# Eight w1 half tiles instead of six, two ReLU tiles instead of one, and raw w1 tiles asked for earlier

## The chip, the cores and the metric

The kernel runs on one core of one Trainium2 chip. The metric is the device time of one execution in microseconds (us), from several runs; the profile is of one execution. The core's engines are TensorE (PE; PEld is its weight load), VectorE (DVE), ScalarE (ACT), GpSimd (POOL) and SyncE (SP), which issues every DMA of this kernel.

## The reference

The input x has 2048 tokens of 512 features. It is normalised, goes through attention with 32 heads of 16 features and, in parallel, through an MLP with 1792 hidden features and squared ReLU, and the two are joined by a gate:

```python
xn = _layernorm(x)
qkv = (xn @ wqkv)                                  # 32 heads of 16
p = softmax(einsum("bhqd,bhkd->bhqk", q, k) * 16 ** -0.5)
s = (p @ v) @ wo
h = relu(einsum("bsd,df->bsf", xn, w1) + b1)       # 1792 hidden
g = silu(einsum("bsf,fd->bsd", h * h, w2) + b2)
return x + s * g
```

All of it is in float32.

## The kernel before, in words

Operands of the large products are split into a high and a low part in a shorter float format (`split`), and each product is the sum of three matmuls, high by high, high by low and low by high (`terms3`). 

Attention goes in 32 units: 8 groups of four heads by 4 blocks of 512 queries. A unit has 16 steps, one for each block of 128 keys, so the main loop has 512 steps, numbered `st`. In a step TensorE makes four score tiles (`exp_mm`, L1123) whose exponentials ScalarE takes (L1130), four score tiles for the row maxima of the unit 24 steps ahead (`max_mm`, L289), each reduced by VectorE (L296), and the P·V product of the step two before (`pv_mm`, L362), which closes the step. The row maxima go through DRAM into two rows of the q tile as a shift (`keep`, `back`). When a unit is done its result is copied out (`evac`, L372), its row sums are gathered by a DMA into a small tile sm (L380), inverted by VectorE (L386), sent through DRAM as a broadcast (L389, L394) and multiplied in by GpSimd (L400 to L402). These six actions stand 1, 4, 5, 7, 9 and 12 steps after the copy.

The MLP is the filling of these steps: the generator `dense()` hands out, step by step, a list of matmuls. It works in 8 chunks of 256 tokens. For each chunk there are 14 tiles of 128 hidden features (`first`, two steps each, in chunk 0; `first_pair`, four steps for two tiles, in chunks 1 to 7), then two token tiles of the second product (`second`, 14 steps each). So the first product of chunk 0 runs in steps 4 to 31, its second product in 32 to 59, and each later chunk takes 56 steps. The results of the first product go through the tile `r`: ScalarE writes the ReLU of two hidden tiles into its halves (L490, L532), GpSimd squares it in place (L493, L535) and splits it into hT (L80, L81). `gate` in `second` uses the same memory for the tanh (`th`, L559 to L561). PSUM has one bank for the MLP (`pd`, one buffer), so a tile's first matmul waits until ScalarE has taken the tile before.

w1 reaches the chip in two ways. In chunk 0 each of the 14 tiles comes as a raw tile (`load_w1`, L433) in a ring of three tiles called ex, is split by GpSimd into two half tiles of the ring w1s (`split_w1`), and stored split in DRAM two steps later (L445). In chunks 1 to 7 the split half tiles come back from DRAM (`load_part`, L455), 28 a chunk. The ring w1s has six half tiles. Six are loaded ahead during the second product of the chunk before; the others are asked for inside `first_pair`, each at the place in TensorE's order where the half tile whose place it takes has been read for the last time (`between`). The raw tiles of w2 use the ring ex after those of w1 (`load_w2`).

In the main loop the order on each engine is the program's order, nothing is reordered. `later(n, fn)` puts an action at the beginning of the step n steps on, and `begin(st)` runs those that are due, ahead of the step's other work. SP issues in order, so a DMA that waits holds up all that stand behind it: the q tiles (L134), the k tiles (L145), the shift rows (L335, L355), the sums, w1, w2 and the MLP's outputs (L563).

Of the kernel before, what the change touches and what calls it, by code (L numbers as in the profile page):

```python
# [8 lines left out]
F32 = mybir.dt.float32  # L9
F32R = mybir.dt.float32r  # L10
# [6 lines left out]
P = 128  # L17
# [22 lines left out]
def kernel(  # L40
# [55 lines left out]
    with ExitStack() as ph:  # L96
# [317 lines left out]
        def mlp_tasks(mp):  # L414
# [4 lines left out]
            rot["ex"] = [ex.tile([P, D], F32, name=f"ex{i}") for i in range(3)]  # L419
            turn["ex"] = 0  # L420
            m1 = ExitStack()
            r = m1.enter_context(tc.tile_pool(name="rp", bufs=1)).tile([P, 2, CW], F32, name="r")
            wr = m1.enter_context(tc.tile_pool(name="wr", bufs=1))
            xp = m1.enter_context(tc.tile_pool(name="xc", bufs=1))
            w2t = wp.tile([P, 2, FO, D], F32R, name="w2t")
            rot["w1s"] = [wr.tile([P, 2, 2, P], F32R, name=f"w1s{i}") for i in range(6)]
            turn["w1s"] = 0

            raws = []
# [46 lines left out]
            def first(c, fo):  # L476
                i = fo % 2
                if fo == 0:
                    state["hT"] = hp.tile([P, 2, FO, CW], F32R, name="hT")
                xc, hT, w = state["xc"], state["hT"], state["w"].pop(0)  # L480
                ps = pd.tile([P, 512], F32, name="pd_t")[:, :CW]
                if fo + 2 < FO:
                    split_w1(fo + 2)
                if fo + 3 < FO:
                    load_w1(fo + 3)
                if fo >= FO - 5:
                    load_w2(fo - FO + 5, 3)

                def post():
                    nc.scalar.activation(r[:, i], ps, AF.Relu, bias=b1_t[:, fo : fo + 1])  # L490
                    if i == 0:
                        return
                    nc.gpsimd.tensor_tensor(r, r, r, op=ALU.mult)  # L493
                    fs = slice(fo - 1, fo + 1)
                    split((hT[:, 0, fs], hT[:, 1, fs]), r)

                return halves(
                    terms3(ps, [
                        (
                            lambda a, q, ko=ko: w[ko // 2][q, a, ko % 2],  # L500
                            lambda b, q, ko=ko: xc[q, b, ko],
                        )
                        for ko in range(KO)
                    ]), (12,), post, 2,
                )

            def first_pair(c, f):

                if f == 0:
                    state["hT"] = hp.tile([P, 2, FO, CW], F32R, name="hT")  # L510
                xc, hT = state["xc"], state["hT"]
                ps = pd.tile([P, 512], F32, name="pd_t")
                mms = []
                for i in range(2):
                    w = state["w"].pop(0)
                    mms += terms3(ps[:, i * CW : (i + 1) * CW], [
                        (
                            lambda a, q, ko=ko, w=w: w[ko // 2][q, a, ko % 2],
                            lambda b, q, ko=ko: xc[q, b, ko],
                        )  # L520
                        for ko in range(KO)
                    ])

                out_, lh, rh, _, last = mms[3 * KO]
                mms[3 * KO] = out_, lh, rh, False, last

                between = {k: load_part for k in (2, 5, 8, 11)}

                def post():
                    for i in range(2):  # L530
                        fo = 2 * f + i
                        nc.scalar.activation(  # L532
                            r[:, i], ps[:, i * CW : (i + 1) * CW], AF.Relu, bias=b1_t[:, fo : fo + 1]
                        )
                    nc.gpsimd.tensor_tensor(r, r, r, op=ALU.mult)  # L535
                    fs = slice(2 * f, 2 * f + 2)
                    split((hT[:, 0, fs], hT[:, 1, fs]), r)

                return block(mms, 2, post, between)

            def second(c, tt):
                hT = state["hT"]
                ps = pd.tile([P, D], F32, name="pd_t")
                u = up.tile([P, D], F32, name="u")
                th = r.rearrange("p a b -> p (a b)")
                ts_ = slice(tt * P, (tt + 1) * P)

                if c == 0 and tt == 0:
                    for k in range(5, FO):
                        later(k - 4, lambda k=k: load_w2(k, 2))  # L550

                def post():
                    nc.scalar.activation(u, ps, AF.Copy)  # L553
                    nc.gpsimd.tensor_tensor(u, u, b2_t, op=ALU.add)  # L554
                    later(2, gate)

                def gate():

                    nc.scalar.activation(th, u, AF.Tanh, scale=0.5)  # L559
                    nc.gpsimd.tensor_scalar(th, th, 0.5, 0.5, op0=ALU.mult, op1=ALU.add)  # L560
                    nc.gpsimd.tensor_tensor(u, u, th, op=ALU.mult)  # L561
                    t0 = c * CW + tt * P
                    later(4, lambda: nc.sync.dma_start(g_d[t0 : t0 + P, :], u))  # L563

                mms = terms3(ps, [
                    (lambda a, q, fo=fo: hT[q, a, fo, ts_], lambda b, q, fo=fo: w2t[q, b, fo])
                    for fo in range(FO)
                ])
                if c == 0:
                    yield from halves(mms, (6,) * 7, post, 1)  # L570
                    return
                if c == NCK - 1 and tt:

                    for i, task in enumerate(halves(mms, (6,) * 7, post, 1)):
                        if i == 4:
                            oldest_first("pt")
                            rot["pt"][:] = [t for t in rot["pt"] if all(t is not x for x in rot["ex"])]
                        yield task
                    return

                if tt:
                    yield from halves(mms[:6], (6,), None, 1)
                    mms = mms[6:]
                for k in range(0, 36, 12):
                    yield from block(mms[k : k + 12], 1, post if tt and k == 24 else None)
                if not tt:
                    yield from halves(mms[36:], (6,), post, 1)
# [4 lines left out]
                load_w1(fo)  # L592
            state["w"] = []
            split_w1(0)
            later(1, lambda: split_w1(1))
            for _ in range(2):
                yield [], None
            for c in range(NCK):
                if c == 1:

                    oldest_first("pt")
                    rot["pt"][:0] = rot["ex"]
                if c == 0:
                    for fo in range(FO):
                        yield from first(c, fo)
                else:
                    for f in range(FO // 2):
                        yield from first_pair(c, f)
                if c + 1 < NCK:
                    load_xc(c + 1)  # L610
                    state["part"] = 0
                    for k in range(6):
                        later(14 + k, load_part)
                else:
                    m1.close()
                    wo_setup()
                for tt in range(CW // P):
                    yield from second(c, tt)
# [292 lines left out]
        def qk_tile(m, c, last=False):  # L911
            ps = pd.tile([P, 512], F32, name="pd_t") if last else pe.tile([P, 512], F32, name="se")
            for out_, lh, rh, first_, last_ in qk_terms(m, c, ps):
                nc.tensor.matmul(out_, lh(slice(0, P)), rh(slice(0, P)), start=first_, stop=last_)  # L914
                if not last_:
                    yield
            if last:

                hl = pools["n"].tile([P, 2, 512], F32R, name="hl")
                raw = sp.tile([P, 512], F32, name="ot", bufs=1)  # L920
                nc.scalar.activation(raw, ps, AF.Copy)
                split((hl[:, 0], hl[:, 1]), raw)
                later(3, lambda: qk_store(m, c, hl))
                yield
                return
            if m % 4 == 0:
                hl = hlp.tile([P, 2, 512], F32R, name="hl")
                split_psum(hl[:, 0], hl[:, 1], ps)
            else:
                hl = hlp.tile([P, 2, 512], F32R, name="hl")  # L930
                raw = hlp.tile([P, 512], F32, name="raw", bufs=2)
                nc.scalar.activation(raw, ps, AF.Copy)
                split((hl[:, 0], hl[:, 1]), raw)
            qk_store(m, c, hl)
            yield
# [388 lines left out]
```

## Time and profile before

| | us |
|---|---|
| median of three runs | 1696.4 |
| lowest and highest run | 1695.42, 1696.55 |
| the profiled execution's own time | 1695.05 |
| its span, first to last instruction | 1693.3 |

| engine | busy us | share of the span |
|---|---|---|
| TensorE matmul | 1660.9 | 98% |
| TensorE weight load | 943.8 | 56% |
| VectorE | 1353.3 | 80% |
| ScalarE | 1192.6 | 70% |
| GpSimd | 519.0 | 31% |

Busy time is the union of an engine's instructions. Matmuls are pipelined and their ends are modelled, so a busy TensorE can still have lost time; a wait shows in the idle time ahead of an instruction and in the distance between the closing groups of two steps. In a timeline a row gives the start in us from the beginning of the span, the duration, the engine (SPq is SyncE's queue of DMA issues), the line, what is written from what, how many, and in brackets the idle time before it with what ended it. The duration of an issue on SP is not that of its transfer; the chain of waits shows transfers from issue to landing where somebody waited for them.

### The profile page before, as it was taken

How to read it: one execution, taken by the hardware profiler on the slowest of the kernel's cores; microseconds unless marked ns; L12 is line 12 of the kernel's file. 1: busy time of each engine (PE TensorE's matmuls, PEld its weight loads, DVE VectorE, ACT ScalarE, POOL GpSimd, SP SyncE). 2: the span in 40 equal slices, each digit the busy share in tenths (PEclk: the TensorE clock that was granted, in tenths of full speed). 3: DMA queues.
4: the chain of work that ended last, by engine and by line, in shares of the span. 5: the costliest groups of instructions: out<-in, count | busy, mean ns of one | idle time of the engine just before them, and what ended most of it. 6: DMA issues, size and time to landing. Idle time of an engine off the chain costs nothing.

```text
span 1693.3 us, 35473 instructions
## 1 busy us (share of the span) xinstructions
PE 1660.9 (98%) x13312; PEld 943.8 (56%) x13312; DVE 1353.3 (80%) x2303; ACT 1192.6 (70%) x2354; POOL 519.0 (31%) x538
## 2 busy tenths in 40 slices
PE   6999999999999999999999999999999999999998
PEld 5766565556545655565466456545655565555533
DVE  6255688888888888888888888888888888887633
ACT  7211577777777777777777777777777777776675
POOL 4335467522212321231133113211221233134322
PEclk9999999999999999999999999999999999999999
DMA  7648566425333433343343334323432352158434
GB/s 281 176 148 269 163 188 191 110 78 139 104 77 92 116 95 86 99 118 80 90 118 94 78 86 142 106 59 97 139 91 76 75 151 72 42 183 231 120 111 137
DMA packets 156315, 207.73 MB, mean 123 GB/s; under 512 B 50992, under 2 KB 70960, under 8 KB 154608
## 3 DMA queue, kind: packets, MB, share of 16 engines
q1 hardware_dynamic: 156144, 205.46, 42.6%
q8 instruction: 105, 1.72, 0.5%
q14 instruction: 66, 0.54, 0.1%
HBM read 149.04 MB, written 56.08 MB: 121 GB/s over the span
## 4 chain that ended last, share of the span: by engine, by line
PE 94%; DMA 2%; DVE 1%; ACT 1%; POOL 1%; issue 0%; SPq 0%; ACTq 0%; DVEq 0%; POOLq 0%
PE po L362 29%; PE pm_t L289 17%; PE pd_t L236 16%; PE se L1123 13%; PE pd_t L204 9%; PE se L914 5%; PE se L945 3%; DMA w1s<-w_d 1%; PE pm_t L814 1%; DVE mx L296 1%; ACT pt L1130 0%; PE pm_t L326 0%; PE pm_t L1123 0%; DMA xc<-xn_d 0%; ACT xn L980 0%
## 5 line engine op out<-in xcount | busy, mean ns | idle before, releaser
L296 DVE TENSOR_REDUCE mx<-pm_t 128x1 f32<-128x512 f32 x2048 | 1275.6, 684 | 241.4 <-PE pm_t L289 142.4
L1130 ACT ACTIVATE pt<-se 128x512 f32<-128x512 f32 x1730 | 902.8, 610 | 258.1 <-PE se L1123 221.5
L289 PE MATMUL pm_t<-ka,qm 64*128 64x512 f32 x2048 | 797.5, 423 | 1.9 <-DVE mx L296 1.6
L1123 PE MATMUL se<-qe,ka 64*128 64x512 f32 x2000 | 686.4, 402 | 0.0
L362 PE MATMUL po<-pt,v 128*32 128x512 f32 x3556 | 545.1, 605 | 0.0
L289 PEld LDWEIGHTS pm_t<-ka,qm 64*128 64x128 f32 x2048 | 352.6, 184 | 276.5 <-DVE mx L296 249.1
L1123 PEld LDWEIGHTS se<-qe,ka 64*128 64x128 f32 x2000 | 339.5, 184 | 21.6 <-issue 5.7
L236 PEld LDWEIGHTS pd_t<-xc,w1s 64*128 64x128 f32 x2352 | 292.4, 187 | 86.4 <-issue 82.2
L236 PE MATMUL pd_t<-xc,w1s 64*128 64x256 f32 x2352 | 333.7, 288 | 2.2 <-DMA w1s<-w_d 2.0
L236 PE MATMUL pd_t<-w2t,hT 64*128 64x512 f32 x936 | 259.9, 410 | 0.0
L236 PEld LDWEIGHTS pd_t<-w2t,hT 64*128 64x128 f32 x936 | 156.1, 184 | 72.3 <-issue 65.4
L362 PE MATMUL po<-ex,v 128*32 128x512 f32 x540 | 192.3, 605 | 0.0
L1130 ACT ACTIVATE ex<-se 128x512 f32<-128x512 f32 x270 | 147.7, 614 | 37.1 <-PE se L1123 30.6
L535 POOL TENSOR_TENSOR r<-r 128x512 f32<-128x512 f32 x49 | 51.0, 1041 | 335.6 <-ACT r L532 335.6
L362 PEld LDWEIGHTS po<-pt,v 128*32 128x32 f32 x3556 | 79.9, 108 | 132.4 <-issue 111.3
L554 POOL TENSOR_TENSOR u<-u,b_t 128x512 f32<-128x512 f32 x16 | 20.6, 1285 | 310.5 <-ACT u L553 310.5
L204 PE MATMUL pd_t<-w2t,hT 64*128 64x512 f32 x408 | 105.5, 391 | 0.0
L204 PE MATMUL pd_t<-wot,oc 64*128 64x512 f32 x336 | 91.0, 407 | 2.9 <-ACT pt L1130 0.9
L400 POOL TENSOR_TENSOR ot<-ot,hl 128x512 f32<-128x512 f32 x30 | 38.5, 1285 | 179.8 <-DMA hl<-r_d 137.1
L204 PEld LDWEIGHTS pd_t<-wot,oc 64*128 64x128 f32 x336 | 58.9, 185 | 47.7 <-DVE mx L296 12.5
L204 PEld LDWEIGHTS pd_t<-w2t,hT 64*128 64x128 f32 x408 | 72.5, 184 | 8.9
L532 ACT ACTIVATE r<-pd_t,b_t 128x256 f32<-128x256 f32 x98 | 41.1, 470 | 51.6 <-PE pd_t L236 51.6
(115 smaller groups left out, 1113.1 us busy)
## 6 DMA issues: line engine op xcount, KB each, us to landing
w1s<-w_d SPq DMA_DIRECT2D x196, 256.0 KB
qm<-q_d SPq DMA_DIRECT2D x384, 32.0 KB
qe<-q_d SPq DMA_DIRECT2D x384, 32.0 KB
ka<-k_d SPq DMA_DIRECT2D x96, 128.0 KB
xn_d<-xT SPq DMA_DIRECT2D x8, 1024.0 KB
k_d<-hl SPq DMA_DIRECT2D x32, 256.0 KB
q_d<-hl SPq DMA_DIRECT2D x32, 256.0 KB
xc<-xn_d SPq DMA_DIRECT2D x16, 512.0 KB
```

What stands on the lines that cost most here:

```text
L204: mm = nc.tensor.matmul(out_, lh(r), rh(r), start=first_ and lane == 0, stop=last_ and lane == 1, skip_group_check=True,)
L236: mm = nc.tensor.matmul(out_, lh(r), rh(r), start=first_ and lane == 0, stop=last_ and lane == 1, skip_group_check=True,)
L289: nc.tensor.matmul(ps, qms[u][p][64 * j : 64 * j + 64, qb * P : (qb + 1) * P], kas[qd, p][64 * j : 64 * j + 64, kc * 512 : (kc + 1) * 512] ...
L296: return nc.vector.tensor_reduce(mxs[u][:, c, kc : kc + 1], ps, axis=AX.X, op=ALU.max)
L362: nc.tensor.matmul(po[32 * j : 32 * j + 32, :], vs[qd][:, (4 * kb + j) * VW : (4 * kb + j) * VW + 32], pts[j], start=(kb == 0), stop=(kb = ...
L400: nc.gpsimd.tensor_tensor(ot, ot, hl[:, 1].bitcast(F32), op=ALU.mult)
L532: nc.scalar.activation(r[:, i], ps[:, i * CW : (i + 1) * CW], AF.Relu, bias=b1_t[:, fo : fo + 1])
L535: nc.gpsimd.tensor_tensor(r, r, r, op=ALU.mult)
L914: nc.tensor.matmul(out_, lh(slice(0, P)), rh(slice(0, P)), start=first_, stop=last_)
L945: nc.tensor.matmul(out_, lh(slice(0, P)), rh(slice(0, P)), start=first_, stop=last_)
L1123: nc.tensor.matmul(se, kas[qd, j // 2][b : b + 64, kb * P : (kb + 1) * P], qes[u][j // 2][b : b + 64, :], start=True, stop=True,)
L1130: return nc.scalar.activation(pts[j], se, AF.Exp, scale=0.25)
```

## The change

There are five edits. The tile `r` becomes two tiles `rs`, used in turn by the pairs of hidden tiles, and by the two token tiles in `gate`. The ring w1s has eight half tiles; eight are asked for ahead, at steps 13 to 20 after the second product begins, instead of six at steps 14 to 19. Inside `first_pair` nothing is edited: the loads there stop by themselves when all 28 are asked for. In chunk 0 a raw tile of w1 is asked for five tiles ahead instead of three, directly behind the split that frees its place; tiles 3 and 4 are asked for one and two steps after the first split. The store of the last k tile, which is computed at the beginning of the main loop, moves from three to six steps after its computation.

```diff
-            r = m1.enter_context(tc.tile_pool(name="rp", bufs=1)).tile([P, 2, CW], F32, name="r")
+            rp = m1.enter_context(tc.tile_pool(name="rp", bufs=1))
+            rs = [rp.tile([P, 2, CW], F32, name=f"r{i}") for i in range(2)]
...
-            rot["w1s"] = [wr.tile([P, 2, 2, P], F32R, name=f"w1s{i}") for i in range(6)]
+            rot["w1s"] = [wr.tile([P, 2, 2, P], F32R, name=f"w1s{i}") for i in range(8)]
...
-                ps = pd.tile([P, 512], F32, name="pd_t")[:, :CW]
+                ps, r = pd.tile([P, 512], F32, name="pd_t")[:, :CW], rs[fo // 2 % 2]
                 if fo + 2 < FO:
                     split_w1(fo + 2)
-                if fo + 3 < FO:
-                    load_w1(fo + 3)
+                if fo + 5 < FO:
+                    load_w1(fo + 5)
...
-                xc, hT = state["xc"], state["hT"]
+                xc, hT, r = state["xc"], state["hT"], rs[f % 2]
...
-                th = r.rearrange("p a b -> p (a b)")
+                th = rs[tt].rearrange("p a b -> p (a b)")
...
-            later(1, lambda: split_w1(1))
+            later(1, lambda: [split_w1(1), load_w1(3)])
+            later(2, lambda: load_w1(4))
...
-                    for k in range(6):
-                        later(14 + k, load_part)
+                    for k in range(8):
+                        later(13 + k, load_part)
...
-                later(3, lambda: qk_store(m, c, hl))
+                later(6, lambda: qk_store(m, c, hl))
```

## The prediction

> **What bounds the kernel now.** I read the page first, then busy time by stretch, then what TensorE waited for in those stretches, and at the end the timeline around each wait. The page's first lines and its chain of waits:
>
> ```profile
> span 1693.3 us, 35473 instructions
> PE 1660.9 (98%) x13312; PEld 943.8 (56%) x13312; DVE 1353.3 (80%) x2303; ACT 1192.6 (70%) x2354; POOL 519.0 (31%) x538
> PE 94%; DMA 2%; DVE 1%; ACT 1%; POOL 1%; issue 0%; SPq 0%; ACTq 0%; DVEq 0%; POOLq 0%
> ```
>
> The chain that ended last is TensorE's own work for 94%. An edit that takes no matmul away can win only what TensorE waits. The diff reaches two stretches: the MLP's first chunk (195 to 290 us), and chunks 1 to 7 (366 to 1412 us). In the table by stretch each engine has its busy us; the last three columns are the granted clock, DMA share and GB/s:
>
> ```profile
> 195.00:290.00 95.00, 90.88 (x852) 56.07 (x856) 79.57 (x133) 71.25 (x141) 64.10 (x91) 1.00 0.63 191
> 366.00:1412.00 1046.00, 1043.78 (x9214) 585.01 (x9206) 922.46 (x1546) 803.56 (x1602) 253.17 (x250) 1.00 0.38 100
> ```
>
> What weight loads (PEld) waited for in the first stretch (first row) and in the second (second row): us in total, times, longest:
>
> ```profile
> PEld pd_t L204 <- ACT r L490: 4.2, 2, 2.3
> PEld pd_t L236 <- DMA w1s<-w_d: 4.0, 5, 1.1
> ```
>
> These 4.2 and 4.0 us are the stake, 8.2 us or 0.48% of the span. The larger sums in the same view (waits for VectorE's maximum, for issue) come from the interleaving of every step, which the diff leaves alone.
>
> Is a wait of TensorE lost time, or slack that is made up later? The P·V group (L362) closes each step; these are its starts around the first 2.3 us wait, the first three rows from TensorE's timeline, the other two from the chain in order of time:
>
> ```profile
> 213.37 1.06 PE L362 MATMUL po<-pt,v 128*32 128x512 f32 x8
> 216.23 1.07 PE L362 MATMUL po<-pt,v 128*32 128x512 f32 x8
> 221.37 1.06 PE L362 MATMUL po<-pt,v 128*32 128x512 f32 x8
> ...
> 224.29 1.01 PE po L362 x8
> 227.20 1.00 PE po L362 x8
> ```
>
> Steps last 2.86 us before, 5.14 with the wait, then 2.92 and 2.91. Nothing is made up, so a wait that goes is worth its length. The Trainium skill's Perfetto Trace Analysis, section Identifying the Most-Contended Engine, calls matmul busy time no measure for TensorE and takes LDWEIGHTS busy time instead. By that rule 56% of the span here would make VectorE, at 80%, the most contended engine, and the gain from these waits would be near zero instead of 8.2 us. The steps after the wait do not bear that out.
>
> **The change part by part.**
>
> First chunk: the raw w1 tiles and the second ReLU tile. The timeline around both 2 us waits, in order of time (idle time and its releaser in brackets):
>
> ```profile
> 209.81 0.55 SPq L433 DMA_DIRECT2D ex<-in_B_w_dram  x1
> 213.73 0.40 POOL L80 TENSOR_SCALAR w1s<-ex 128x256 fp32r<-128x256 f32 x1 [7.93 <-DMA ex<-in_B_w_dram]
> 216.10 1.04 POOL L493 TENSOR_TENSOR r<-r 128x512 f32<-128x512 f32 x1
> 217.92 1.26 POOL L81 TENSOR_TENSOR hT<-r,hT 128x512 fp32r<-128x512 f32 x1
> 219.22 0.47 ACT L490 ACTIVATE r<-pd_t,b_t 128x256 f32<-128x256 f32 x1 [2.22 <-POOL hT L81]
> 219.74 0.18 PEld L204 LDWEIGHTS pd_t<-xc,w1s 64*128 64x128 f32 x1 [2.33 <-ACT r L490]
> ...
> 279.08 0.47 ACT L490 ACTIVATE r<-pd_t,b_t 128x256 f32<-128x256 f32 x1 [1.78 <-POOL hT L81]
> ```
>
> Raw tile 3 is asked for at 209.81, so GpSimd stands 7.93 us before it can split it; the squaring of the first pair queues behind that split, its last reader of r ends at 219.18, and only then may ScalarE write the next ReLU into the same r. The PSUM bank has one buffer, so TensorE waits with it. The second wait has the same end but another start: GpSimd, busy for 64 of this stretch's 95 us, is behind with splits of w1 and w2 and with the normalisation of a finished unit.
>
> With two r tiles in turn, ReLU 2 writes the other tile and does not wait for the first pair; ReLU 12 waits for the pair before last, whose split of hT stands four steps (11 us) earlier. That alone removes both waits: -4.2 us. What is late next is the consumer of hT, the second matmul, which begins after the chunk and reads the last pair in the last of its seven parts; a lag of GpSimd of a few us there costs nothing. Without that cover GpSimd's backlog would be paid in full, 1.8 us.
>
> Raw tile 3 now goes out a step after the first split. Ahead of it on SP stand these:
>
> ```profile
> 200.95 5.71 SPq L134 DMA_DIRECT2D qm<-q_d  x12
> 206.76 2.01 SPq L900 DMA_DIRECT2D k_d<-hl  x2
> 208.86 0.90 SPq L445 DMA_DIRECT2D w_d<-w1s  x2
> ```
>
> It goes behind the first six of the twelve qm loads, at 200.95 + 2.85 = 203.8, and with the 213.73 - 209.81 = 3.9 us that it took before it lands near 207.7, 6 us sooner. The two w1s tiles it needs are the two added ones. The k_d store moves three steps back and its 2.01 us with it; its readers come five head groups later. I count nothing extra for this: the same 4.2 us go either way.
>
> The cost: each later raw load (L433, five ahead) now takes the place of the tile split in the same step, so SP stands until GpSimd has finished that split, and everything behind it on SP stands too. The tightest thing behind it is the sum row of the first finished unit (sm, L380), which VectorE's reciprocal needs at a fixed place in its order:
>
> ```profile
> 239.03 0.44 SPq L433 DMA_DIRECT2D ex<-in_B_w_dram  x1
> 241.71 0.73 POOL L81 TENSOR_TENSOR w1s<-ex,w1s 128x256 fp32r<-128x256 f32 x1
> 240.19 2.68 SPq L134 DMA_DIRECT2D qe<-q_d  x6
> 243.39 2.62 SPq L134 DMA_DIRECT2D qm<-q_d  x6
> 246.11 2.67 SPq L445 DMA_DIRECT2D w_d<-w1s  x2
> 248.87 0.62 SPq L380 DMA_DIRECT2D sm<-ot  x1
> 251.36 0.24 DVE L386 RECIPROCAL sm<-sm 128x16 f32<-128x16 f32 x1
> 1544.86 1.91 DMA sm<-ot
> ```
>
> The row of 1544.86, from the chain, is the only one that shows how long such a transfer takes when VectorE stands waiting: 1.91 us. In the first chunk it has 251.36 - 248.87 = 2.49 us, a slack of 0.6. After the change the raw load of 239.03 waits for the split that ends at 241.71 + 0.73 = 242.44, 3.4 us later. Behind it: the load and a ka load (0.5 us each), six qe (2.7), six qm (2.6), two w1 stores (0.90 as at 208.86, or 2.67 as here) put sm at 249.7 to 251.5 and its landing at 251.6 to 253.4 (the first wait's 2.3 us shift all of this alike). VectorE then waits 0.2 to 2.0 us. Below that lies 0, if SP made up the rest; I take 1.0, since the short store is the commoner row, and charge it to TensorE in full, though three PSUM banks for the maxima can hide some. The shift rows of units 1 and 2 stand behind the same waits, but are needed six steps (17 us) after they are asked for, against SP waits like these 3.4 us. Cost: +1.0 (0 to 2.0).
>
> Chunks 1 to 7: eight half tiles. SP's timeline ahead of one of the five waits, then that wait, and two of the four w1s transfers of such length that stand in the chain, the first and the longest:
>
> ```profile
> 706.21 2.75 SPq L134 DMA_DIRECT2D qm<-q_d  x6
> 709.78 1.84 SPq L455 DMA_DIRECT2D w1s<-w_d  x4
> 712.60 0.18 PEld L236 LDWEIGHTS pd_t<-xc,w1s 64*128 64x128 f32 x1 [1.04 <-DMA w1s<-w_d]
> ...
> 709.78 2.78 DMA w1s<-w_d
> 1077.89 3.39 DMA w1s<-w_d
> ```
>
> SP issues without a gap from 706.2 to 711.6 (q tiles of the next unit), so the half tile whose place came free in the third step of the pair goes out at 709.78 and lands 2.78 us later, 1.04 too late. With six tiles it is wanted as third half of the next pair, some two steps (6 us) after its place is free; with eight as first half of the pair after, some five and a half steps (16 us). Ten us more against a lateness of at most 1.1 us removes all five waits: -4.0 us. The number of loads stays 28 a chunk: eight instead of six ahead, none instead of two in the sixth pair. The two added ones stand at the ends of this stretch of SP, shown for chunk 3's loads:
>
> ```profile
> 642.91 0.42 SPq L455 DMA_DIRECT2D w1s<-w_d  x1
> 651.57 2.91 SPq L134 DMA_DIRECT2D qe<-q_d  x6
> ```
>
> SP is idle from 643.3 to 651.6, so an issue of 0.42 us is free there; the other end is after the qm loads, with the next unit's need steps away. Zero, at most 2 x 0.42 us a chunk if SP were full. The two r tiles change nothing here: GpSimd is busy 253 of 1046 us.
>
> Sum: -4.2 - 4.0 + 1.0 = -7.2 us on the profiled execution's 1695.05, which gives 1687.9. That execution lies 1.3 us under the median of the runs, 1696.4; I predict 1696.4 - 7.2 = 1689.2 us.
>
> **The rivals.** *Half of it stays.* Either the w1s loads are still late, or GpSimd's lag still reaches TensorE. For it: SP stays the one queue of all loads. Against it: the margins above, 10 us against 1.1, and a second tile against a single dependence. It gives 1696.4 - 4.2 + 1.0 = 1693.2, or with the other half 1693.4.
>
> *Waits are slack.* VectorE is busy 922 of 1046 us in the second stretch and takes the waits' place; 1696.4. For it: 88% is not far from full. Against it: the steps after the wait. The Trainium skill's rule above leads here too.
>
> *Slower, by SP's queue in the first chunk.* If SP, standing behind the raw loads, falls so far behind that the sum row and the shift rows come late, VectorE and then TensorE stand. The seven even-numbered tiles each have such a wait of about 3 us. It decides only when its cost passes the 8.2 us gained and the 3.4 us that can be told, so 11.6 us, as when all seven cost 2 us: 1696.4 - 8.2 + 14 = 1702. Against it: the w1 stores wait for the same splits now, two steps later, and the only such wait of TensorE in the first stretch is the 4.2 us named above.
>
> **How the numbers follow.** A difference under 0.2%, 3.4 us, cannot be told from no change. My forecast, 1686.5 to 1691.5: 0.70. More than that, since a small wait on VectorE also goes: 0.03. Half: 0.11. No change: 0.11. Slower: 0.05. The half case lies a hair inside 0.2% at 1693.2; I put most of it on the faster side with its cost under 1.0. Faster 0.82, same 0.13, slower 0.05. The range runs from 1686.0 (the gain without cost is 1688.2, and 2 us for waits of VectorE and ScalarE that end with it) to 1694.0, which takes in the half case.
>
> **What would show it.** Right: no row of TensorE waiting for r L490 or for w1s in the two stretches; the GpSimd wait of 7.93 us before the fourth split gone; steps of 2.9 us throughout 195 to 290. The cost shows as a VectorE wait of sm L386 for its DMA near 249 us. Wrong: w1s rows among TensorE's waits again, SP waiting long for GpSimd's w1s with q tiles or shift rows behind it, or steps that stay as long with another releaser named.

## The result and the profile after

| | before | after |
|---|---|---|
| median of 11 runs, us | 1696.39 | 1689.70 |
| lowest and highest run | 1694.08, 1698.16 | 1686.06, 1693.10 |
| ratio to before | | 0.996 (95%: 0.9951 to 0.997) |
| profiled execution, its own time | 1695.05 | 1688.97 |
| its span | 1693.3 | 1687.2 |

The change is 0.4% faster, 6.7 us by the medians and 6.1 us between the two profiled executions. The first lines of the page of the changed kernel and its chain:

```profile
span 1687.2 us, 35420 instructions
PE 1658.8 (98%) x13312; PEld 944.1 (56%) x13312; DVE 1352.7 (80%) x2303; ACT 1192.5 (71%) x2354; POOL 520.3 (31%) x538
PE 96%; DVE 1%; DMA 1%; ACT 1%; SPq 0%; issue 0%; DVEq 0%; ACTq 0%
```

The work of each engine is what it was; TensorE's share of the chain rises from 94% to 96%. In TensorE's waits of the two stretches neither the row for `r` nor the row for w1s is left. What replaces them is a wait of VectorE in the first chunk (195 to 286 us: total, times, longest), with the largest wait of TensorE that can be put down to the changed lines, from the same stretch:

```profile
DVE sm L386 <- DMA sm<-ot: 1.6, 1, 1.6
PEld pd_t L204 <- POOL w1s L80: 0.2, 1, 0.2
```

The starts of the P·V groups show where the 6.1 us went. The first four rows are from the chain, in order of time, around the place of the old 5.14 us step; the other three are from TensorE's timeline, around unit 0's inverse:

```profile
214.05 0.99 PE po L362 x8
216.90 1.02 PE po L362 x8
219.80 1.02 PE po L362 x8
222.66 1.03 PE po L362 x8
...
248.74 1.07 PE L362 MATMUL po<-pt,v 128*32 128x512 f32 x8
252.72 0.64 PE L362 MATMUL po<-pt,v 128*32 128x512 f32 x4
255.76 1.06 PE L362 MATMUL po<-pt,v 128*32 128x512 f32 x8
```

The steps are now 2.85, 2.90 and 2.86 us where one lasted 5.14; and step 21, which lasted 2.88 before, lasts 252.72 - 248.74 = 3.98. Laid side by side over all 512 steps, the two profiles differ in a few steps and agree to about 0.2 us in the others: -2.24 and -1.78 for the two waits of the first chunk, +1.10 for step 21 and +0.16 for the step after it, -1.07, -0.52, -1.42 and -1.20 in chunks 3, 4, 5 and 7. That is 7.0 us less in the steps that the change reaches. Two things lie outside the changed lines: the loop's first P·V group starts 0.64 us later, and step 468 is 0.63 us longer. With 0.3 us less at the end this is the 6.1 us. Steps are numbered here as the kernel numbers them, each ending with its P·V group (the first is in step 2); the recorded expectations below call step 468, that of unit 28's inverse, st 467.

### The profile page after: what moved, and what is told of

The parts are those of the page before. It is cut to its first block, busy times and chain, and to the rows that moved or that the text cites. A ratio compares the mean times of both kernels' runs of the same rounds, so it can differ in the third digit from the quotient of the medians.

```text
span 1687.2 us, 35420 instructions
## 1 busy us (share of the span) xinstructions
PE 1658.8 (98%) x13312; PEld 944.1 (56%) x13312; DVE 1352.7 (80%) x2303; ACT 1192.5 (71%) x2354; POOL 520.3 (31%) x538
## 4 chain that ended last, share of the span: by engine, by line
PE 96%; DVE 1%; DMA 1%; ACT 1%; SPq 0%; issue 0%; DVEq 0%; ACTq 0%
PE po L362 30%; PE pm_t L289 17%; PE pd_t L236 17%; PE se L1125 12%; PE pd_t L204 9%; PE se L916 5%; PE se L947 3%; DVE mx L296 1%; PE pm_t L1125 0%; PE pm_t L816 0%; PE pm_t L326 0%; DMA xt<-in_A_x_dram 0%; DMA xc<-xn_d 0%; ACT pt L1132 0%; DMA wm<-in_A_wqkv_dram 0%
```

## The experiments

The runs were on several chips, on which the median of the kernel before was 1692.8 to 1696.4 us, so times are given as ratios to the kernel before on the same chip, and the mechanism is read from the steps and waits of each profile. Steps are compared with those of the first profile of the kernel before, shown ahead of the prediction.

### Each part alone

**Two ReLU tiles alone.**

```diff
-            r = m1.enter_context(tc.tile_pool(name="rp", bufs=1)).tile([P, 2, CW], F32, name="r")
+            rp = m1.enter_context(tc.tile_pool(name="rp", bufs=1))
+            rs = [rp.tile([P, 2, CW], F32, name=f"r{i}") for i in range(2)]
...
-                ps = pd.tile([P, 512], F32, name="pd_t")[:, :CW]
+                ps, r = pd.tile([P, 512], F32, name="pd_t")[:, :CW], rs[fo // 2 % 2]
...
-                xc, hT = state["xc"], state["hT"]
+                xc, hT, r = state["xc"], state["hT"], rs[f % 2]
...
-                th = r.rearrange("p a b -> p (a b)")
+                th = rs[tt].rearrange("p a b -> p (a b)")
```

> The kernel before with two ReLU tiles in turn and nothing else. Theory: the wait of ReLU for the pair before is the one dependence behind both 2 us waits of the first chunk, so the row PEld pd_t L204 waiting for r L490 (4.2 us) goes, though GpSimd still stands about 8 us for raw tile 3; the 4.0 us for w1s in chunks 1 to 7 stay; no VectorE wait for the sums in the first chunk. About 4 us less, 1692.3. Rival (the late raw tile is the cause, the tile r only passes it on): the first wait stays at about 2 us in another row, and the gain is about 2 us.

Measured: ratio 0.9974 (0.9963 to 0.9985). Both waits of the first chunk are gone, by 2.24 and 1.80 us (2.24 and 1.78 in the changed kernel), and step 21 is as short as before. The waits for w1s, expected to stay at 4.0 us, are 2.3 us in this profile. GpSimd's and ScalarE's timelines at the old place:

```profile
213.46 0.41 POOL L80 TENSOR_SCALAR w1s<-ex 128x256 fp32r<-128x256 f32 x1 [7.19 <-PE se L1124]
217.65 1.28 POOL L81 TENSOR_TENSOR hT<-r,hT 128x512 fp32r<-128x512 f32 x1
217.43 0.50 ACT L491 ACTIVATE r<-pd_t,b_t 128x256 f32<-128x256 f32 x1
```

GpSimd still stands 7.19 us before it splits tile 3 (the releaser that the profile names is inferred). But ReLU 2 starts at 217.43, before the last reader of the first pair has begun; in the kernel before it had to wait for that reader's end. So the shared tile was the dependence that reached TensorE; the late raw tile only made it long.

**Eight half tiles alone.**

```diff
-            rot["w1s"] = [wr.tile([P, 2, 2, P], F32R, name=f"w1s{i}") for i in range(6)]
+            rot["w1s"] = [wr.tile([P, 2, 2, P], F32R, name=f"w1s{i}") for i in range(8)]
...
-                    for k in range(6):
-                        later(14 + k, load_part)
+                    for k in range(8):
+                        later(13 + k, load_part)
```

> The kernel before with eight w1 half tiles, eight asked for ahead, and nothing else. Theory: the 4.0 us of waits for w1s in chunks 1 to 7 go, both waits of the first chunk (4.2 us) stay as they are; about 4.2 us less, 1692.2. Rival (the waits are slack or pass to VectorE): no gain, 1696.4.

Measured: ratio 0.9989 (0.998 to 0.9998). No wait for w1s is left, and the four steps of chunks 3, 4, 5 and 7 are shorter by 1.08, 0.52, 1.41 and 1.20 us, together 4.2, as expected. The waits of the first chunk stay, at 3.5 us. The time shows less than half of the 4.2 (the medians differ by 1.6 us). In this profile step 468 is 1.28 us longer than in the kernel before and the loop starts 1.2 us later; that this is what the medians lost is not shown. Step 468 is taken up below.

**The raw tiles alone**, with one ReLU tile and six half tiles.

```diff
-                if fo + 3 < FO:
-                    load_w1(fo + 3)
+                if fo + 5 < FO:
+                    load_w1(fo + 5)
...
-            later(1, lambda: split_w1(1))
+            later(1, lambda: [split_w1(1), load_w1(3)])
+            later(2, lambda: load_w1(4))
...
-                later(3, lambda: qk_store(m, c, hl))
+                later(6, lambda: qk_store(m, c, hl))
```

> The kernel before with the raw tiles asked for five ahead and the k store moved, with one ReLU tile and six half tiles. Theory: raw tile 3 is asked for near 204 instead of 210, so the first wait of the first chunk (2.2 us) goes and the second (1.8 us), which comes from GpSimd's backlog, stays; the sums of the first unit come late behind the raw load, VectorE stands 1 to 2 us for them and TensorE pays about 1.1; the 4.0 us for w1s stay. Net 1 us less, 1695.3, hardly to be told from before. Rival (asking early is what removes both waits): 3 us less, 1693.3.

Measured: ratio 1.0 (0.9992 to 1.0008). The first wait goes (-2.26 us), step 21 gets 1.13 us longer, and of the second wait 1.2 us stay:

```profile
PEld pd_t L204 <- ACT r L490: 1.2, 1, 1.2
```

So this part alone does what was expected, but that some of the second wait goes too (its step is 0.73 us shorter); it gives back nearly half of what it wins, and its time cannot be told from no change.

**The two others without it.** The changed kernel with the three raw-tile edits undone.

> The changed kernel with the raw tiles asked for three ahead and the k store where they were before, so two ReLU tiles and eight half tiles alone. Theory: both gains of 4 us without the cost of 1.1, about 1 us faster than the changed kernel, 1688.4; no VectorE wait for sm L386 near 249 us, and GpSimd's wait of 8 us is back without a wait of TensorE. Rival (the early raw tiles are needed once the waits are gone): a wait of TensorE for w1s or r returns in the first chunk, 1 to 2 us slower than the changed kernel, 1691.

Measured: ratio 0.9975 (0.9965 to 0.9985). The mechanism is as expected: both gains are there in the steps, step 21 lasts as long as in the kernel before (VectorE waits 0.33 us for the sums), no wait for `r` or w1s returns. The time does not show it: on this chip two ReLU tiles alone won 4.1 us by the medians, eight half tiles alone 1.6, and both together 3.4, although the steps add up. In this profile steps 468 and 469 last 5.7 and 5.1 us, 3.15 us more than in the kernel before. The kernels do not differ there. This made a second place suspect. Of the 3.15 us, 1.71 stand in step 468, where VectorE waits; in step 469, where the other 1.44 us stand, the granted clock was 0.50, and 1.00 ahead of it. In these rows by stretch it is the third number from the end:

```profile
1541.00:1544.00 3.00, 1.48 (x9) 0.34 (x9) 2.33 (x5) 0.03 (x1) 0.00 (x0) 1.00 0.82 262
1544.20:1547.40 3.20, 3.09 (x14) 2.47 (x16) 1.56 (x4) 1.71 (x3) 0.00 (x0) 0.50 0.53 152
```

### What the raw loads cost, and by which way

In the changed kernel SP's timeline ahead of step 21, with GpSimd's split that it waits for and VectorE's inverse:

```profile
237.13 0.81 SPq L446 DMA_DIRECT2D w_d<-w1s  x2
240.14 0.73 POOL L81 TENSOR_TENSOR w1s<-ex,w1s 128x256 fp32r<-128x256 f32 x1
240.90 0.38 SPq L434 DMA_DIRECT2D ex<-in_B_w_dram  x1
241.93 2.67 SPq L134 DMA_DIRECT2D qe<-q_d  x6
244.69 3.73 SPq L134 DMA_DIRECT2D qm<-q_d  x6
249.46 0.62 SPq L380 DMA_DIRECT2D sm<-ot  x1
251.44 0.25 DVE L386 RECIPROCAL sm<-sm 128x16 f32<-128x16 f32 x1 [1.56 <-DMA sm<-ot]
```

SP stands from 237.9 until the split ends at 240.87, and the sums go out at 249.46, 1.98 us before VectorE can use them. Two edits to the changed kernel, each of which breaks one link of this.

**Four tiles ahead**, so that the place was freed two steps before and SP has nothing to wait for:

```diff
-                if fo + 5 < FO:
-                    load_w1(fo + 5)
+                if fo + 4 < FO:
+                    load_w1(fo + 4)
...
-            later(2, lambda: load_w1(4))
```

> The changed kernel with each raw tile asked for four tiles ahead, where its place was freed by the split of the step pair before, so that SP has nothing to wait for; raw tile 3 still goes out a step after the first split. Theory: the cost of the change is SP's stand behind the split alone; VectorE's wait for the first unit's sums is under 0.5 us, the step of the inverse (st 21) lasts 2.9 us instead of 3.98, and GpSimd does not wait 8 us for raw tile 3; about 1.1 us less than the changed kernel. Rival (the sums are late because the early raw loads crowd SP and the DMA engines): the step stays near 4 us, no gain.

Measured: ratio 0.9976 (0.9967 to 0.9984). SP and VectorE at the same place:

```profile
246.39 0.62 SPq L380 DMA_DIRECT2D sm<-ot  x1
249.16 0.24 DVE L386 RECIPROCAL sm<-sm 128x16 f32<-128x16 f32 x1
```

The sums go out 2.77 us ahead of the inverse, VectorE does not wait, and step 21 lasts 2.90 us. GpSimd waits 4.7 us in all for raw tiles of w1 (3.9 in the changed kernel, 10.9 in the kernel before). The raw loads are still early here, so the stand behind the split was the cause. The time does not show the 1.1 us: the changed kernel was not run beside it, and its two measurements gave 0.996 and 0.9977.

**The inverse two steps later**, with SP standing as in the changed kernel:

```diff
-            steps = EVAC_LAST if u >= 28 else EVAC
+            steps = EVAC_LAST if u >= 28 else (1, 6, 7, 9, 11, 14) if u == 0 else EVAC
```

> The changed kernel with the inverse of the first unit's sums, and the actions after it, two steps later. SP still stands behind the splits. Theory: TensorE pays for SP's stand only by way of that inverse, so step 21 lasts 2.9 us and the first chunk has no longer step in its place; about 1.1 us less than the changed kernel. Rival (others behind SP, shift rows or q tiles, are as late): another step of the first chunk is 1 us longer, no gain.

Measured: ratio 0.9967 (0.9955 to 0.9979). Step 21 lasts 2.88 us and no other step of the first chunk is longer in its place. TensorE paid through this one inverse, and nothing else behind SP was late enough.

### The second place: unit 28's sums

In every profile so far VectorE waits near 1540 us for the sums of unit 28, in a stretch where SP also issues the loads of the last phase. The rows, from VectorE's timelines of the changed kernel, of the kernel without the raw-tile edits, and of the changed kernel once more (below):

```profile
1541.13 0.25 DVE L386 RECIPROCAL sm<-sm 128x16 f32<-128x16 f32 x1 [2.38 <-DMA sm<-ot]
```

```profile
1541.67 0.25 DVE L386 RECIPROCAL sm<-sm 128x16 f32<-128x16 f32 x1 [3.45 <-DMA sm<-ot]
```

```profile
1539.76 0.25 DVE L386 RECIPROCAL sm<-sm 128x16 f32<-128x16 f32 x1 [1.83 <-DMA sm<-ot]
```

Unit 28 has the shorter plan of steps (1, 3, 4, 5, 7 and 9 after the copy), in which the inverse stands two steps behind the request for the sums, and not three. The edit puts the inverse and each action after it two steps later.

```diff
-            steps = EVAC_LAST if u >= 28 else EVAC
+            steps = (1, 5, 6, 7, 9, 11) if u == 28 else EVAC_LAST if u > 28 else EVAC
```

> The changed kernel with the inverse of unit 28's sums, and the actions after it, one step to two steps later. In all profiles so far VectorE stands 1.7 to 3.5 us for these sums near 1540 us and the step there (st 467) lasts 3.99 to 5.70 us. Theory: this is the same dependence at a second place, and it varies from run to run with SP's queue, which is what blurs the gain in the times; the step lasts 3.3 to 3.7 us in every profile, 1 us less than the changed kernel. Rival (the step is set by other work, the wait is slack): 4 us or more remain, no gain.

Measured: ratio 0.9964 (0.9951 to 0.9976), median 1686.4 us with the runs within 1686.07 to 1687.27. VectorE does not wait; step 468 lasts 3.39 us (4.62 in the changed kernel), step 469 3.33 (3.66). The P·V groups that bound these two steps, first in the changed kernel, then here:

```profile
1537.79 1.07 PE L362 MATMUL po<-pt,v 128*32 128x512 f32 x8
1542.41 1.07 PE L362 MATMUL po<-pt,v 128*32 128x512 f32 x8
1546.07 1.06 PE L362 MATMUL po<-pt,v 128*32 128x512 f32 x8
```

```profile
1537.97 1.07 PE L362 MATMUL po<-pt,v 128*32 128x512 f32 x8
1541.35 1.06 PE L362 MATMUL po<-pt,v 128*32 128x512 f32 x8
1544.69 1.06 PE L362 MATMUL po<-pt,v 128*32 128x512 f32 x8
```

Step 21 is 3.97 us, as it must be, since the raw loads are untouched. The price of this wait can be read from all profiles together. In the eleven in which VectorE waits here, for 1.74 to 4.74 us, step 468 is 2.2 to 2.4 us longer than that wait (1.74 and 3.99, 2.38 and 4.62, 3.45 and 5.70, 4.74 and 7.13); in the three without the wait it lasts 3.4. So about the first 1.1 us of the wait are hidden and the rest is paid one for one.

**The kernel before, once more.**

> The kernel before, once more, for a second profile. Theory: the waits of the first chunk (4.2 us) come from an order of instructions and stay to 0.1 us; the w1s waits depend on when DMAs land and vary by 1 us or more around 4.0, as does the step of unit 28's sums. Rival: all of them are fixed.

Measured: one execution of 1698.92 us, above the 17 others of this kernel on the same chip (1690.27 to 1696.43). TensorE's waits for w1s in its chunks 1 to 7, and the largest of them in the chain:

```profile
PEld pd_t L236 <- DMA w1s<-w_d: 5.2, 6, 1.8
```

```profile
434.75 5.11 DMA w1s<-w_d
```

Step 84, which had no such wait in the other profile, lasts 5.76 us here, 2.18 more, behind a w1s transfer of 5.11 us. The next one lasts 3.51, 1.38 more; the granted clock was 0.50 there for 3.4 us. So the w1s waits do vary, as theory had it, and eight half tiles are what leaves none: in the four profiles with six they are 4.0, 2.3, 3.3 and 5.2 us, and with eight there is none in any. The waits of the first chunk vary too, against it: the two long steps last 4.65 and 4.00 us here, not 5.14 and 4.68, and the row for `r` is 3.0 us instead of 4.2. The order of instructions makes them possible; their length is the lead of TensorE over GpSimd. Here the loop began 0.6 us later and TensorE lost 0.81 us more in step 4, where it waits for its tokens (xc); so it came to the first place 1.4 us later than in the other profile. GpSimd's last reader of `r` ended only 0.9 us later, and the step is 0.49 us shorter.

### Together, and the depth of the ring

**Four ahead and the later inverse of unit 28**, on top of the changed kernel:

> The changed kernel with each raw tile asked for four tiles ahead and with unit 28's inverse later, the two edits that each took a wait for the sums away. Theory: both waits of VectorE for the sums are gone, every step of the first chunk lasts 2.9 us and step 467 3.4 us; 1 us less than with the later inverse of unit 28 alone and 3 us less than the changed kernel, 0.995 to 0.996 of before. Rival (the two have a common cause elsewhere): one of the two waits returns, no faster than with either edit alone.

Measured: median 1684.35 us against 1692.79 for the kernel before, ratio 0.9953 (0.9938 to 0.9968). No VectorE wait for sums is left in the profile; step 21 and step 468 last 2.88 and 3.38 us. Page and chain:

```profile
span 1681.6 us, 35432 instructions
PE 97%; DVE 1%; ACT 1%; DMA 1%; issue 0%; SPq 0%; DVEq 0%; ACTq 0%
```

**The same without any of the raw-tile edits**: two ReLU tiles, eight half tiles and the later inverse of unit 28.

> Two ReLU tiles, eight half tiles and the later inverse of unit 28, with the raw tiles asked for three ahead and the k store where they were before. Theory: the early raw tiles contribute nothing once there are two ReLU tiles; the same time as with four ahead, within 0.5 us, and GpSimd's wait of 8 us for raw tile 3 stands without a wait of TensorE. Rival (the early raw tile gives GpSimd a needed lead): 1 us or more slower, with a wait of TensorE in the first chunk.

Measured: median 1684.2, ratio 0.9951 (0.9937 to 0.9965). The same. GpSimd stands up to 7.5 us for a raw tile and TensorE does not wait. Once there are two ReLU tiles the earlier raw tiles win nothing.

**Seven half tiles** in the changed kernel.

> The changed kernel with seven half tiles, seven asked for ahead. The first half tile asked for in a pair is then wanted as fourth half of the next pair, under 1 us later than with six; the other three are wanted in the pair after. Theory (waits are the lateness of that first half tile, at most 1.1 us, against the lead of the ring): part of the 4.0 us is left, between 0.2 and 2 us. Rival (any deeper ring will do, since a seventh tile takes the burst off SP): 0.

Measured in one execution: of the four longer steps one is left, step 308, which lasts 3.79 us instead of 3.57 with eight tiles and 5.00 with six. That is 0.2 us, the lower end of what was expected, and too near 0 for one profile to refute the rival; the profile names no wait for w1s there, so that it is the rest of the old one is read from its place. One tile more is nearly enough; eight leave nothing.

**The changed kernel once more**, beside these:

> The changed kernel once more, beside the others on one chip. Theory: steps 21 and 467 are long again (4.0 us, and 4.5 to 6), and the time lies 2 to 4 us above the version with both inverses freed. Rival (the differences of the sums are chance): one of the two steps is short here.

Measured: ratio 0.9977 (0.9968 to 0.9986), median 1689.56. So the change wins 3.2 us in this measurement, where it won 6.7 in the first; the intervals of the two ratios hardly meet. Step 21 lasts 4.05 us; step 468 lasts 4.07, less than the 4.5 expected, with VectorE waiting 1.83 us. The best two versions are 5.3 us faster than the changed kernel on the same chip, more than the 2 to 4 us expected. The profiled executions of the changed kernel and of the version with four ahead lie 4.0 us apart; of these the inverses account for 1.3 (steps 21 and 22) and 1.0 (468 and 469). Another 1.6 us stand in steps 498 and 499, which no edit touches: in the changed kernel's profiles the granted clock falls to 0.50 there for 3.4 us, in the other it does not. The first row is from the changed kernel's first profile, the second from the version with four ahead, at the same place:

```profile
1636.20:1639.40 3.20, 3.20 (x16) 0.79 (x12) 0.36 (x1) 2.07 (x4) 0.00 (x0) 0.50 0.02 5
1632.00:1635.20 3.20, 3.20 (x25) 1.79 (x25) 0.68 (x3) 2.06 (x4) 0.00 (x0) 1.00 0.02 5
```

## Why the prediction was right

The forecast was 1689.2 us, the median is 1689.7. That they agree to 0.5 us is partly luck: the forecast starts from the median of the kernel before in the same measurement, and measured once more the change won 3.2 us and not 6.7. What bears the mechanism is the steps: 7.0 us less where the change reaches, against 7.2 forecast. By its steps:

- *Waits are worth their length.* Right. Each wait that went shortened its own step by about that much, and the steps between kept their length. (The prediction's 2.92 and 2.91 us for the steps after a wait mix starts of two views that differ by 0.05 us; in one view they are 2.87 and 2.89.) The rival by which the waits are slack falls. By the Trainium skill's Perfetto Trace Analysis (Identifying the Most-Contended Engine), taken with the share of weight loads alone, VectorE would be the limit, since weight loads fill only 56%; the trace does not agree: their share is still 56% and the time is gone. The page names MFU, the share of the peak arithmetic rate that the matmuls reach, beside that share; the prediction left it out, and no run here shows it.
- *Two r tiles, -4.2.* Right in place and size: -2.24 and -1.78 us; alone they do the same. Raw tile 3 was forecast to go out at 203.8 and to land near 207.7; it went out at 204.43 and its split began at 207.51. That the raw tile is a second way to the same gain was half wrong: early raw tiles alone end the first wait, and 1.2 us of the second stay.
- *Eight half tiles, -4.0.* Right: -4.2 us over the four steps, alone and together. The size is that of one profile: the waits that went vary from 2.3 to 5.2 us with six half tiles. The preload of eight cost nothing that shows.
- *The cost, +1.0 (0 to 2.0).* Right in place, and near in size partly by luck. The sums were forecast to go out between 249.7 and 251.5, less the shift of 2.3, so between 247.4 and 249.2; they went out at 249.46, in a loop that began 0.64 us later, behind six q tiles (qm) that took 3.73 us instead of the 2.6 assumed. VectorE waited 1.56 us, more than the 1.0 taken, and TensorE paid 1.10 in step 21 and 0.16 in the next, less than the full wait that it was charged; the two errors cancel for the most part.
- *What was missed.* Unit 28's sums wait in the same way, in both kernels, and the row of 1544.86 that gave the price of such a transfer was itself that wait. The prediction used it as a price and did not ask what set it. It costs 0.6 us more in the profile after than in that before, and it varies more than the cost that was weighed. The granted clock was not asked about beyond the two stretches of the change, where it is 1.00.
- *The slower rival*, SP falling far behind, needed several late transfers; there was one. The later inverse shows that nothing else behind SP was late enough.

## What to carry to other kernels

When a wait passes through several hands (a late load, a split, a squaring, a shared tile, a PSUM bank), look for the one dependence that reaches the engine that sets the time; giving that tile a second buffer ended both waits here, while the late load stayed and cost nothing. A prefetch that takes its place from work issued in the same step makes the queue wait for that work, with everything behind it; asking one tile less far ahead kept the prefetch and lost the wait. And a transfer that has just enough time is a coming wait: look through the profile for its siblings before pricing one of them.

## What the runs showed that was not expected

The same dependence can be worth different amounts on the same program: unit 28's sums made VectorE wait 1.7 and 2.6 us in two profiles of the kernel before, 2.4 and 1.8 in two of the changed kernel, 3.5 without the raw-tile edits and 4.7 with unit 0's later inverse, where step 468 lasted 7.13 us. The w1s transfers that TensorE waited for took 2.75 to 3.39 us in one profile of the kernel before; in the other one took 5.11 and the rest 2.69 to 2.83. A change that removes such a wait wins more in some executions than in others, so a comparison of two profiles and one of medians can differ by a few us. The version without both waits for sums still had single runs 4 to 5 us above its fastest, so not all of the spread comes from them.

Much of what is left goes with the granted clock. Each execution has a mean granted clock. The changed kernel's first eleven runs have medians of 1687.5 us at 0.998 (four runs), 1689.7 at 0.997 (three), 1691.5 at 0.996 (two) and 1692.7 at 0.995 (two), and the runs 4 to 5 us above the fastest of the version with four ahead are those at 0.997 and 0.995, the four others being at 0.998. In the profiles the lower clock stands in stretches of mostly 3.4 or 6.8 us at 0.50 (3.4 us at half the clock take about 0.001 off the mean). Some lie in the last 20 us of every profile. The others make a step, or two together, 1.0 to 1.6 us longer: step 469 without the raw-tile edits, with unit 0's later inverse and in the second profile of the kernel before, step 85 in that profile, and steps 498 and 499 in eight of the fourteen profiles (3.1 us where the stretch is of 6.8).

The first four each begin at the end of a step in which TensorE was held up, or within 2 us after it. That such a hold-up sets the stretch off is not shown: with eight half tiles alone VectorE waited 3.03 us for unit 28's sums and the clock stayed at 1.00. If it does, a wait can cost more than its length, and that may be why freeing unit 28's inverse won more in the medians than in the steps.
